# Decode attention with a cache: three loads of the output weights move from ScalarE's DMA queue to SyncE's

## The chip, the core and the metric

The kernel runs on one NeuronCore of one Trainium2 chip. The metric is the device time of one execution in microseconds (us), as the median of several runs. TensorE (PE) does the matmuls, VectorE (DVE), ScalarE (ACT) and GpSimd (POOL) the elementwise work, and SyncE (SP) issues DMAs. ScalarE can issue DMAs too. Each of the two has a DMA queue of its own, and both queues are served by the same 16 DMA engines.

## The reference

32 sequences of 4 new tokens each attend to a cache of 2048 positions. There are 32 query heads of 128 elements, and 4 key and value heads, each shared by 8 query heads. All data are bfloat16.

```python
B, Sq, D = 32, 4, 1024
Hq, Hkv, Sk, Dh = 32, 4, 2048, 128
def reference(x, k_cache, v_cache, wq, wo):
    q = (x @ wq).reshape(B, Sq, Hq, Dh).transpose(0, 2, 1, 3)
    k = jnp.repeat(k_cache, 8, axis=1)
    v = jnp.repeat(v_cache, 8, axis=1)
    scores = jnp.einsum("bhqd,bhkd->bhqk", q, k) * (Dh ** -0.5)
    p = softmax(scores, axis=-1)
    o = jnp.einsum("bhqk,bhkd->bhqd", p, v)
    return o.transpose(0, 2, 1, 3).reshape(B, Sq, Hq * Dh) @ wo
```

The caches are 64 MiB each, wq and wo 8 MiB each; the result y is 128 rows of 1024.

## The kernel before

Three stages follow one another. First x and the four loads of wq come in, and TensorE computes all queries. Then a loop goes over the 32 batches: 2 MiB of keys and 2 MiB of values are loaded, VectorE transposes the keys (`kt`, L333), TensorE computes the scores (`pe_qk`, L346 and the helper at L16) and, three batches later, the weighted values (`pe_pv`, L399, 64 matmuls); ScalarE does the exponentials (L359) and the scaling of the result into `QT_sb` (`o_evac`, L408). Last comes the output projection: VectorE turns the results into `oT_sb` (`o_turn`, L415), TensorE multiplies them with wo head by head (`oproj`, 32 heads, each in three matmuls of 512, 288 and 224 columns: the first of a head is at L425, the others at L16; for the last two heads the 512 columns come first and the rest after), VectorE and ScalarE copy the sums to `y_sb` (L437, L439), and two DMAs store the halves of y (L444), the first issued by SyncE, the second by ScalarE.

A small program object, `_Program`, keeps one list of operations for each engine. An operation stands in its engine's list in the order in which the Python code adds it, with the semaphores that it waits for; an engine does its list strictly in order. So SyncE's list is x, wq, then all loads of keys and values in the order of the list `loads` (L211), then loads of wo (L228), then the first store.

The loads of keys and values go to seven slots of the tensor `big`, four for values and three for keys. wo is loaded into four of these slots once they are free: heads 0 to 7, 8 to 15 and 16 to 23 into the slots of the keys of batches 29, 30 and 31, free when VectorE has transposed these keys (`("kt", b, 1)`), and heads 24 to 31 into the slot of the values of batch 28, free when TensorE has used them (`("pv", 28)`). The loads, `pieces`, are numbered 0 to 13 by the variable `c`: six of four heads (1 MiB), two of two heads, two of one head, and four halves of a head for the last two heads.

Which queue a load of wo takes is chosen at L228:

```python
load = ("act" if c in (1, 3, 5) else "sp", lambda e, dst=dst, src=src: e.dma_start(dst, src),
        [("kt", b, 1) if kind == "k" else ("pv", b)], ("wo", c), f"s_wo{c}")
```

Loads 1, 3 and 5 are kept aside in `act_loads`, and are added to ScalarE's list in the batch loop, right after the scaling of batch 30 (`o_evac(j)` with `j == L - 1`, where `L` is 31). The others are added to SyncE's list behind all loads of keys and values. In `oproj` each matmul waits for the load that brings its weights, `("wo", piece)`, and for the last `o_turn`.

Of the kernel before, what the change touches and what calls it, by code (L numbers as in the profile page):

```python
# [103 lines left out]
def bass_standalone__gqa_block_cached__sampling_kernel(  # L104
# [41 lines left out]
    with ExitStack() as es:  # L146
# [31 lines left out]
        def ps_q(j):  # L178
            return ps_s[:, 512 * j:512 * (j + 1)] if j < 4 else ring[j - 4]

        def words(ap):
            return ap.bitcast(F32)

        p = _Program()
# [18 lines left out]
        for kind, b in loads:  # L203
# [6 lines left out]
            src = (k_cache if kind == "k" else v_cache)[b].rearrange("g (r t) d -> (g r) t d", r=R)  # L210
# [4 lines left out]
        def wo_at(u, m):  # L215
            return big[:, wo_slot[u // 8], :, :].rearrange("p t d -> p (t d)")[:, u % 8 * D:(u % 8 + m) * D]
# [1 line left out]
        wo_v = wo.rearrange("(h p e) n -> p h (e n)", p=128, e=4)  # L218
        pieces = [(sum(WO[:c]), m, 0, D) for c, m in enumerate(WO)] + [(Hq - 2, 1, 0, NA), (Hq - 1, 1, 0, NA), (Hq - 2, 1, NA, D), (Hq - 1, 1, NA, D)]
        assert sum(WO) == Hq - 2  # L220
        act_loads = []
        for c, (u, m, n0, n1) in enumerate(pieces):
            assert u // 4 == (u + m - 1) // 4
            kind, b = wo_for[u // 8]
            dst, src = wo_at(u, m), wo_v[:, u // 4, u % 4 * D:(u % 4 + m) * D]
            if m == 1:
                dst, src = dst[:, n0:n1], src[:, n0:n1]
            load = ("act" if c in (1, 3, 5) else "sp", lambda e, dst=dst, src=src: e.dma_start(dst, src),  # L228
                    [("kt", b, 1) if kind == "k" else ("pv", b)], ("wo", c), f"s_wo{c}")
            if c in (1, 3, 5):  # L230
                act_loads.append(load)
            else:
                p.dma(*load)


        p.op("pool", lambda e: e.memset(ident[:], 0.0), [], "ident0")
# [17 lines left out]
        def pe_idle(n, out_, rhs, waits=()):  # L254
            for c in range(n):
                if c == 0:
                    mm = lambda e: e.matmul(out_, lhsT=ident[:, :], rhs=rhs, start=True, stop=True, skip_group_check=True)  # L257
                else:
                    mm = lambda e: _matmul_held(
                        nc, e, out_, ident[:, :], rhs, tile_size=(128, 128), tile_position=(0, 0), start=True, stop=True)  # L260
                p.op("pe", mm, waits if c == 0 else [])
# [17 lines left out]
        for n, j in enumerate(QJ):  # L279
            g, y = j // 2, j % 2  # L280
            dst = q_sb.rearrange("p (x y) a g e -> p x y a g e", y=2)[:, :, y, :, g, :]
            src = ps_q(j).rearrange("p (h a e) -> p h a e", h=4, a=2)
# [8 lines left out]
        for m in range(4):  # L291
# [6 lines left out]
            for a in range(2):  # L298
                src = ring[m].rearrange("p (h a b s) -> p h a b s", h=2, a=2, b=B)[:, :, a, 0:QB, :]
                dst = words(QT_sb[:, 0:QB, a, 2 * m:2 * m + 2, :, :].rearrange("p b h s w -> p b h (s w)"))  # L300
                dst = dst.rearrange("p b h s -> p h b s")
                p.op("dve", lambda e, s=src, d=dst: e.tensor_copy(d, s), [("qt", m)], ("qa", m, a))  # L302
        for m in range(4):
            for a in range(2):
                src = ring[m].bitcast(BF16).rearrange("p (h a b s) -> p h a b s", h=2, a=2, b=B)[:, :, a, QB:, :]
                dst = QT_sb[:, QB:, a, 2 * m:2 * m + 2, :, :].rearrange("p b h s w -> p h b (s w)")
# [20 lines left out]
        def kt(i, chunks):  # L327
            for c in chunks:
                ts = slice(KC * c, KC * (c + 1))
                src = words(big[:, slot_of("k", i), ts, :].rearrange("p t d -> p (t d)"))  # L330
                dst = words(KT_sb[:, i % 2, ts, :, :, :].rearrange("p t a r w -> p (t a r w)"))
                waits = [("k", i)] + ([("qk", i - 2)] if i > 1 else ["qt_all"] if i == 1 else [])
                p.op("dve", lambda e, s=src, d=dst: e.transpose(d, s), waits, ("kt", i, c), gives="t_kt" if c else None)  # L333

        def pe_qk(i):
            waits = [] if i else [("qs", j) for j in range(8)]
            takes = [("t_kt", 1), ("t_pool", 1)] + [("t_exp", 1)] * (i > 0)
            for a in range(2):
                for w in range(2):
                    for c in range(NCH):  # L340
                        out_ = ps_s[:, 512 * c:512 * (c + 1)]
                        lhsT = QD_sb[:, i % 2, a, :, :, w].rearrange("p g q -> p (g q)")
                        rhs = KT_sb[:, i % 2, TC * c:TC * (c + 1), a, :, w]
                        first, last = (a, w) == (0, 0), (a, w) == (1, 1)
                        if c == 0:
                            mm = lambda e, a_=(out_, lhsT, rhs), f=first, l=last: e.matmul(  # L346
                                a_[0], lhsT=a_[1], rhs=a_[2], start=f, stop=l, skip_group_check=True)
                        else:
                            mm = lambda e, a_=(out_, lhsT, rhs), f=first, l=last: _matmul_held(
                                nc, e, *a_, tile_size=(128, 128), tile_position=(0, 0), start=f, stop=l)  # L350
                        p.op("pe", mm, waits, ("qk", i) if last and c == NCH - 1 else None, takes)
                        waits, takes = [], []

        def softmax_max(i):
            p.op("dve", lambda e: e.tensor_reduce(  # L355
                negmx[:, i % 4:i % 4 + 1], ps_s[:, :], AX.X, ALU.max, negate=True), [("qk", i)], ("negmx", i))

        def softmax_exp(i):
            p.op("act", lambda e: e.activation(  # L359
                P_sb[:, :, :, :].rearrange("p t r w -> p t w r"), ps_s[:, :].rearrange("p (t w r) -> p t w r", w=2, r=R),  # L360
                ACT.Exp, bias=negmx[:, i % 4:i % 4 + 1], accum_out=ssum[:, i % 4:i % 4 + 1]),
                [("negmx", i)] + ([("pt", i - 1)] if i else ["qproj"]), ("exp", i))
            p.give("act", ("exp", i), "t_exp")

        def pt(i):
            src = words(P_flat)
            dst = words(PT_sb[:, i % PB, :, :, :].rearrange("p t q w -> p (t q w)"))
            p.op("dve", lambda e: e.transpose(dst, src), [("exp", i)], ("pt", i))  # L368

        def pe_sum(i):  # L370
            p.op("pe", lambda e: e.matmul(ring[(i if i == L else i // 2 * 2) % 4][:, 510 + i % 2:511 + i % 2], lhsT=permf[:, :], rhs=ssum[:, i % 4:i % 4 + 1], start=True, stop=True),  # L371
                 ["permf"] if i == 0 else [], ("ss", i), [("t_exp", 1)] * (i == L))

        def recip(i):
            n = 1 if i >= L - 1 else 2
            src = ring[i % 4][:, 510 + i % 2:510 + i % 2 + n]
            p.op("dve", lambda e: e.reciprocal(rinv[:, i % 4:i % 4 + n], src), [("ss", i + n - 1)], ("rinv", i))
            if n == 2:
                p.at["rinv", i + 1] = p.at["rinv", i]
# [24 lines left out]
        def o_evac(i):  # L404
            buf = ring_of["o", i]
            dst = QT_sb[:, i, :, :, :, :].rearrange("p a h s w -> p (a h s w)").rearrange("p (a d w) -> p a d w", a=2, w=2)
            src = buf[:, 0:Dh].rearrange("p (d a w) -> p a d w", a=2, w=2)
            p.op("act", lambda e: e.activation(dst, src, ACT.Copy, scale=rinv[:, i % 4:i % 4 + 1]), [("pv", i), ("rinv", i)], ("o", i))  # L408
# [38 lines left out]
        L = B - 1  # L447
# [8 lines left out]
        for i in range(B + LAG):  # L456
            j = i - LAG
            starts.append(len(p.ops["pe"]))
            if i < L:
                kt(i + 1, (0,))  # L460
            if i < B:
                pe_qk(i)
                softmax_max(i)
            if 0 < i < B:
                pe_sum(i - 1)
            if i < B:
                pe_idle(20 if i < LAG else 5, ring[j % 4][:, 0:IDLE], idle_rhs, [("qb", 3, 1), ("qs", 3)] if i == 0 else [])
                softmax_exp(i)
            if 0 < i < B and i % 2 == 0:
                recip(i - 2)  # L470
            if i == L:
                recip(L - 1)
            if i < L:
                kt(i + 1, (1,))
            if i < B:
                pt(i)
            if j >= 0:
                for t in range(T):
                    pe_pv(j, t)
                if i == B:  # L480
                    pe_sum(L)
                o_evac(j)
                if j == L - 1:
                    for load in act_loads:
                        p.dma(*load)
            if i == B:
                recip(L)
            if 0 < i <= B:
                pd(i - 1)
            if i + 2 < B:  # L490
                qd(i + 2)
# [65 lines left out]
```

## Time and profile before

| what | value |
|---|---|
| median of 3 runs | 366.52 us (365.57, 366.52, 366.57) |
| the profiled execution | 366.52 us |
| its span, from the first instruction to the last | 364.7 us |
| busy: PE, DVE, ACT, POOL | 308.2, 269.5, 102.6, 165.3 us |
| mean DMA rate over the span | 416 GB/s |
| bytes read from HBM | 151.26 MB |
| loads of wo issued by SyncE | 11 |
| loads of wo issued by ScalarE | 3, 1024 KB each, median 13.7 us to landing |

All times of events are counted from the start of the span. A row of the timeline has the start, the length, the engine, the line, the operation, the tiles (written <- read), the count, and in brackets the idle time of the engine before it and what ended it. "SPq" and "ACTq" are the DMA issues of SyncE and ScalarE; their length is the time of issuing, not of the transfer. A row of the table by stretches has the window, its length, then the busy time and the count of instructions of PE, of PE's weight loads, DVE, ACT and POOL, then the granted clock of TensorE (1.00 is full speed), the busy share of the DMA engines and the rate.

### The profile page before, as it was taken

Reading aid. Unit: us, or ns where it says so; the run is one execution under the profiler, and the core shown is the slowest. Engines: PE = TensorE matmul, PEld = TensorE weight load, DVE = VectorE, ACT = ScalarE, POOL = GpSimd, SP = SyncE. Lnnn points to the kernel's source line nnn. Section 1 sums busy time; section 2 is a strip of 40 time slices with the busy share of each in tenths; the row PEclk is TensorE's granted clock in tenths of the full one; section 3 lists DMA queues with packets and bytes.
Section 4 is the critical chain, followed back from the end, with each engine's and each line's share of the span. In section 5 each row is a group of like instructions: output and inputs, shape, how many; then the busy total and the mean of one; then the engine's idle time right before and its main releaser. Section 6 shows DMA issues by size and latency. Waiting matters only on the chain. (4 is left out here: it accounts for less than half of the span.)

```text
span 364.7 us, 6248 instructions
## 1 busy us (share of the span) xinstructions
PE 308.2 (85%) x3030; PEld 147.2 (40%) x2340; DVE 269.5 (74%) x171; ACT 102.6 (28%) x110; POOL 165.3 (45%) x262
## 2 busy tenths in 40 slices
PE   1988788999999999988998888888888888899586
PEld 1002000445544555544544444444444433469411
DVE  0018799998899999879999888888888888856201
ACT  1014222333333333333333333333332332223000
POOL 8002055355555555555555544444445555543000
PEclk9999999999999999999999999999999999999989
DMA  8999999999999999999999999999999999999992
GB/s 325 431 431 428 426 429 429 431 429 426 423 426 426 429 429 424 430 431 428 431 426 429 423 429 426 429 429 431 428 431 428 428 431 424 426 429 419 420 407 75
DMA packets 12251, 151.66 MB, mean 416 GB/s; under 512 B 1360, under 2 KB 2128, under 8 KB 2768
## 3 DMA queue, kind: packets, MB, share of 16 engines
q1 hardware_dynamic: 11664, 148.25, 95.9%
q10 hardware_dynamic: 576, 3.28, 2.2%
q8 instruction: 6, 0.10, 0.1%
q14 instruction: 5, 0.04, 0.0%
HBM read 151.26 MB, written 0.26 MB: 415 GB/s over the span
## 5 line engine op out<-in xcount | busy, mean ns | idle before, releaser
L333 DVE STREAM_TRANSPOSE KT_sb<-big 128x2048 f32<-128x2048 f32 x64 | 146.6, 2293 | 16.1 <-DMA big<-in_k_cache_dram 16.1
L359 ACT ACTIVATE P_sb<-ps_s,negmx 128x2048 bf16<-128x2048 f32 x32 | 82.1, 2566 | 184.5 <-DVE negmx L355 184.5
L16 PE MATMUL ps_s<-KT_sb,QD_sb 128*128 128x512 bf16 x384 | 103.7, 377 | 0.0
L390 POOL COPY PD_sb<-PT_sb 32x1024 f32<-32x1024 f32 x62 | 64.1, 1034 | 63.2 <-PE ps_r L399 60.4
L390 POOL COPY big<-PT_sb 32x1024 f32<-32x1024 f32 x61 | 63.0, 1034 | 58.7 <-PE ps_r L399 56.0
L355 DVE TENSOR_REDUCE negmx<-ps_s 128x1 f32<-128x2048 f32 x32 | 73.2, 2288 | 12.4 <-PE ps_s L16 10.8
L399 PE MATMUL ps_r<-big 128*128 128x128 bf16 x1024 | 59.8, 219 | 11.6 <-PEq L85 11.6
L399 PE MATMUL ps_r<-big,PD_sb 128*128 128x128 bf16 x1024 | 59.8, 219 | 9.9 <-PEq L85 9.9
L399 PEld LDWEIGHTS ps_r<-big 128*128 128x128 bf16 x1024 | 57.9, 98 | 22.3 <-issue 21.9
L399 PEld LDWEIGHTS ps_r<-big,PD_sb 128*128 128x128 bf16 x1024 | 58.0, 98 | 21.1 <-issue 20.6
L346 PE MATMUL ps_s<-KT_sb,QD_sb 128*128 128x512 bf16 x128 | 48.3, 377 | 17.9 <-PEq L85 17.9
L346 PEld LDWEIGHTS ps_s<-KT_sb,QD_sb 128*128 128x128 bf16 x128 | 12.4, 96 | 102.6 <-issue 102.6
L368 DVE STREAM_TRANSPOSE PT_sb<-P_sb 128x1024 f32<-128x1024 f32 x32 | 39.8, 1245 | 15.8 <-ACT P_sb L359 15.8
L323 POOL COPY QD_sb<-QT_sb 32x64 f32<-32x64 f32 x128 | 29.4, 230 | 46.3 <-DVE QT_sb L302 20.6
L16 PE MATMUL ps_r<-ident 128*128 128x384 bf16 x173 | 33.3, 325 | 0.0
L371 PEld LDWEIGHTS ps_r<-ssum,permf 128*128 128x128 f32 x64 | 11.9, 187 | 24.8 <-issue 23.1
L408 ACT ACTIVATE QT_sb<-ps_r,rinv 128x128 bf16<-128x128 f32 x32 | 11.7, 367 | 29.7 <-PE ps_r L399 27.5
L284 DVE TENSOR_SCALAR KT_sb<-ps_r 128x512 bf16<-128x512 f32 x2 | 1.3, 686 | 20.2 <-PE ps_r L268 20.2
L425 PE MATMUL ps_s<-big,KT_sb 128*128 128x512 bf16 (+1 forms) x32 | 12.6, 405 | 3.3 <-DMA big<-in_wo_dram 3.3
L439 DVE CAST P_sb<-ps_s 128x512 bf16<-128x512 f32 (+1 forms) x2 | 1.0, 536 | 18.9 <-PE ps_s L425 18.9
L16 PE MATMUL ps_s<-big,KT_sb 128*128 128x224 bf16 (+1 forms) x62 | 12.9, 291 | 1.2 <-DVE KT_sb L415 1.1
L257 PE MATMUL ps_r<-ident 128*128 128x384 bf16 x32 | 10.3, 322 | 0.0
(41 smaller groups left out, 85.1 us busy)
## 6 DMA issues: line engine op xcount, KB each, us to landing
big<-in_k_cache_dram SPq DMA_DIRECT2D x32, 2048.0 KB, 18.5
big<-in_v_cache_dram SPq DMA_DIRECT2D x32, 2048.0 KB, 22.0
big<-in_wq_dram SPq DMA_DIRECT2D x4, 2048.0 KB, 14.2
big<-in_wo_dram SPq DMA_DIRECT2D x3, 1024.0 KB, 21.1
big<-in_wo_dram ACTq DMA_DIRECT2D x3, 1024.0 KB, 13.7
big<-in_wo_dram SPq DMA_DIRECT2D x2, 512.0 KB, 23.7
big<-in_wo_dram SPq DMA_DIRECT2D x2, 256.0 KB, 25.1
big<-in_wo_dram SPq DMA_DIRECT2D x4, 128.0 KB, 23.4
```

Source lines behind the costliest of these rows:

```text
L16: return eng.add_instruction(mybir.InstMatmult(name=nc.get_next_instruction_name(), engine=eng.engine, start_tensor_calc=start, stop_tenso ...
L323: p.op("pool", lambda e, s=src, d=dst: e.tensor_copy(d, s), waits if g == 0 else [("pt", i - 2)] * (g == 1 and i > 1), ("qd", i) if g == G ...
L333: p.op("dve", lambda e, s=src, d=dst: e.transpose(d, s), waits, ("kt", i, c), gives="t_kt" if c else None)
L346: mm = lambda e, a_=(out_, lhsT, rhs), f=first, l=last: e.matmul(a_[0], lhsT=a_[1], rhs=a_[2], start=f, stop=l, skip_group_check=True)
L355: p.op("dve", lambda e: e.tensor_reduce(negmx[:, i % 4:i % 4 + 1], ps_s[:, :], AX.X, ALU.max, negate=True), [("qk", i)], ("negmx", i))
L359: p.op("act", lambda e: e.activation(P_sb[:, :, :, :].rearrange("p t r w -> p t w r"), ps_s[:, :].rearrange("p (t w r) -> p t w r", w=2, r=R),
L368: p.op("dve", lambda e: e.transpose(dst, src), [("exp", i)], ("pt", i))
L371: p.op("pe", lambda e: e.matmul(ring[(i if i == L else i // 2 * 2) % 4][:, 510 + i % 2:511 + i % 2], lhsT=permf[:, :], rhs=ssum[:, i % 4:i ...
L390: p.op("dve" if i >= B - 2 and g < i - B + 4 else "pool", lambda e, s=src, d=dst: e.tensor_copy(d, s), [free] * (g == 0 or i >= B - 2) + [ ...
L399: p.op("pe", lambda e: e.matmul(buf[:, 0:Dh], lhsT=pd_of(i)[:, t // 2, :, :, :, t % 2].rearrange("p x g q -> p (x g q)"), rhs=big[:, slot_ ...
L408: p.op("act", lambda e: e.activation(dst, src, ACT.Copy, scale=rinv[:, i % 4:i % 4 + 1]), [("pv", i), ("rinv", i)], ("o", i))
L425: mm = lambda e, a=(out_, lhsT, rhs): e.matmul(a[0], lhsT=a[1], rhs=a[2], start=(u == 0), stop=(u == Hq - 1), skip_group_check=True)
```

## The change

The three loads 1, 3 and 5 are issued by SyncE, in their places between the others, and ScalarE's list no longer has them. What each load waits for, where it writes and who waits for it stay the same. The store of the second half of y is issued by ScalarE in both kernels.

```diff
-        act_loads = []
         for c, (u, m, n0, n1) in enumerate(pieces):
             assert u // 4 == (u + m - 1) // 4
             kind, b = wo_for[u // 8]
             dst, src = wo_at(u, m), wo_v[:, u // 4, u % 4 * D:(u % 4 + m) * D]
             if m == 1:
                 dst, src = dst[:, n0:n1], src[:, n0:n1]
-            load = ("act" if c in (1, 3, 5) else "sp", lambda e, dst=dst, src=src: e.dma_start(dst, src),
-                    [("kt", b, 1) if kind == "k" else ("pv", b)], ("wo", c), f"s_wo{c}")
-            if c in (1, 3, 5):
-                act_loads.append(load)
-            else:
-                p.dma(*load)
+            p.dma("sp", lambda e, dst=dst, src=src: e.dma_start(dst, src),
+                [("kt", b, 1) if kind == "k" else ("pv", b)], ("wo", c), f"s_wo{c}")
...
                 o_evac(j)
-                if j == L - 1:
-                    for load in act_loads:
-                        p.dma(*load)
```

## The prediction

> **What bounds the kernel now.** I read the chain that ended last on the page first, then the chain for the last 29 us, then the timeline, the clock and transfer table and the DMA issues for the same stretch. The chain of 336 to 365 us:
>
> ```profile
> by line: DMA big<-in_wo_dram 35.7%; PE ps_s L425 23.6%; PE ps_s L16 23.0%; PE ps_r L399 4.9%; DVE P_sb L439 2.4%; DVEq L146 1.0%; issue 0.5%; ACT QT_sb L408 0.0%
> ...
> 337.44 10.36 DMA big<-in_wo_dram
> ```
>
> The longest piece is one load of wo that ScalarE issues at 337.44 and that lands 10.36 us later, at 347.8. The timeline says who waits for it:
>
> ```profile
> 322.47 18.74 SPq L228 DMA_DIRECT2D big<-in_wo_dram  x11
> ...
> 337.44 1.37 ACTq L228 DMA_DIRECT2D big<-in_wo_dram  x3
> ...
> 342.92 0.38 PE L16 MATMUL ps_s<-big,KT_sb 128*128 128x288 bf16 x2 [1.10 <-DVE KT_sb L415]
> ...
> 347.85 0.39 PE L425 MATMUL ps_s<-big,KT_sb 128*128 128x512 bf16 x1 [3.25 <-DMA big<-in_wo_dram]
> ```
>
> TensorE begins the output projection at 342.9, does the four heads of the first load, and stands still for 3.25 us until the second load, ScalarE's first, has landed. The table by stretches (us, busy time and count of each engine, granted clock, DMA share, GB/s) shows what follows:
>
> ```profile
> 13.70:27.00 13.30, 11.73 (x54) 0.68 (x7) 1.39 (x3) 1.17 (x3) 0.00 (x0) 1.00 1.01 434
> ...
> 338.00:340.90 2.90, 2.82 (x51) 2.85 (x52) 1.17 (x3) 0.00 (x0) 0.00 (x0) 1.00 1.02 427
> 340.90:344.80 3.90, 2.59 (x28) 1.12 (x18) 0.30 (x2) 0.37 (x1) 0.00 (x0) 1.00 1.01 416
> 344.80:348.20 3.40, 0.35 (x3) 0.10 (x1) 0.00 (x0) 0.00 (x0) 0.00 (x0) 1.00 1.02 422
> 348.20:351.60 3.40, 3.40 (x15) 0.59 (x5) 0.00 (x0) 0.00 (x0) 0.00 (x0) 0.50 1.02 419
> 351.60:355.30 3.70, 3.70 (x26) 0.90 (x9) 0.00 (x0) 0.00 (x0) 0.00 (x0) 0.99 0.99 390
> 355.30:358.00 2.70, 2.65 (x19) 0.59 (x6) 0.00 (x0) 0.00 (x0) 0.00 (x0) 1.00 0.58 200
> ```
>
> The stretch after the pause has a granted clock of 0.50: 3.4 us of work done at half speed costs a further 1.7 us. TensorE never waits again and ends last, while the DMA engines are full (share about 1) only until 355 and empty at 358. So the tail pays 3.25 + 1.7 = 4.95 us, not because bytes are missing, but because they come in the wrong order: while the second load is outstanding, SP's queue brings loads that are needed later. The DMA view of 342 to 344 shows the two queues sharing equally:
>
> ```profile
> q10 hardware_dynamic: 51, 0.42, 50.1%
> q1 hardware_dynamic: 57, 0.40, 48.1%
> ```
>
> q10 is ScalarE's queue (it has nothing before 340 us), q1 SP's.
>
> **What is removed and moved.** Number the loads of wo 0 to 13. Loads 1, 3 and 5 (1 MB each, heads 4-7, 12-15, 20-23) go from ScalarE to SP, each between its neighbours. The store of the second half of y is on ScalarE's queue in both kernels; the diff leaves it alone.
>
> On ScalarE three issues go (1.37 us from 337.44). They lie between the scaling of batch 30 and that of batch 31 at 341.85, which waited for TensorE, so that saves nothing.
>
> On SP three issues are added. Its row is 0.43 us for one (issue starts 322.47, 322.94 and 323.42): 3 x 0.47 = 1.4 us. They fall behind load 0 at 322.47 and end by about 325.3. The slots they write were read out by the transposes of keys 29 to 31, the last of which ended at 320.4, so they don't wait. Load 6 waits for the values of batch 28 until 330.09, and SP stands idle before it:
>
> ```profile
> SPq L228 <- PE ps_r L399: 6.2, 1, 6.2
> ```
>
> So the 1.4 us hides in 6.2 us; with that cover gone it would still stand some 15 us ahead of the first landing that could feel it. Nothing of k or v stands behind these issues.
>
> SP then meets a fuller queue. Three of its late issues take far longer than 0.43 us: those that start at 332.71, 335.39 and 337.54 take 2.64, 2.10 and 3.67 us. About ten loads are then issued and not landed (v of batches 30 and 31 and eight of wo at 332.71). With three more ahead, this begins at load 8 (331) instead of load 11. If each later issue waits for one landing, loads 8 to 13 go out at about 333, 338, 340, 343, 345 and 348. The last one's data are wanted at 357.8, so 10 us are spare: cost nothing.
>
> **When each load lands.** The value rows of batch 31 land at 322.10 + 15.8 = 337.9 and load 0 at 322.47 + 17.8 = 340.3; neither changes, as what stands ahead of them doesn't. From 340.3 the queue brings the loads in order. The rate is the row of 338 to 340.9, where SP's queue alone brings rows of this size: 427 GB/s, 2.46 us per 1,048,576 bytes. For the last six loads I keep the steps between landings of before (issue start plus time to landing gives 355.3, 355.9, 356.6, 357.0, 357.3, 357.6, 357.9 for loads 7 to 13). TensorE's pace is one head per 0.434 us (352.58, 353.01, 353.44 in the timeline), a start 0.05 us after a landing (347.80 to 347.85).
>
> | load | heads | lands | TensorE free | starts |
> |---|---|---|---|---|
> | 0 | 0-3 | 340.3 | 342.9 | 342.9 |
> | 1 | 4-7 | 342.8 | 344.7 | 344.7 |
> | 2 | 8-11 | 345.2 | 346.4 | 346.4 |
> | 3 | 12-15 | 347.7 | 348.1 | 348.1 |
> | 4 | 16-19 | 350.1 | 349.9 | 350.2 |
> | 5 | 20-23 | 352.6 | 351.9 | 352.6 |
> | 6, 7 | 24-27 | 353.8, 355.1 | 354.4 | 354.4 |
> | 8, 9 | 28, 29 | 355.8, 356.4 | 356.1 | 356.1 |
> | 10, 11 | 30, 31, first 512 columns | 356.8, 357.1 | 357.0 | 357.2 for 31 |
> | 12, 13 | 30, 31, the rest | 357.4, 357.75 | 357.4 | 357.8 for 31 |
>
> Both limits meet at the end: without any wait TensorE would start that last piece at 356.6, and the loads allow 357.8. What is late next is therefore the transfer itself.
>
> ```profile
> 361.46 0.99 DVE L439 CAST P_sb<-ps_s 128x512 bf16<-128x512 f32 x2 [18.90 <-PE ps_s L425]
> 361.48 0.29 PE L425 MATMUL ps_s<-big,KT_sb 128*128 128x288 bf16 x1
> ...
> 362.53 0.35 ACTq L444 DMA_DIRECT2D out_dram<-P_sb  x1
> ```
>
> Before, that last piece starts at 361.48: 3.7 us later. The first 512 columns of head 31 go from about 361.2 to 357.2, 4.0 us. The second store waits for two casts in a row on VectorE, of which the first follows the 512 columns: I take 3.9. The profiled execution took 366.52 us, which is the median itself: a span of 364.7 and 1.8 around it. 366.52 - 3.9 = 362.6.
>
> Bounds of the one unknown, the rate of one queue: at the whole span's mean of 416 GB/s the 7.34 MB after load 0 take 0.5 us longer (363.1); at 390, the row of 351.6 to 355.3, 1.6 us longer (364.2). A faster queue ends at TensorE's own limit, 361.48 - 356.6 = 4.9 less: 361.6.
>
> [...]
>
> For the clock my row is the first stage. From 13.7 to 27 us TensorE waits for a load twice (0.26 and 1.26 us), is busy 88%, and keeps a granted clock of 1.00. The table above has pauses of at most 0.7 us and some 90% busy.
>
> **The rivals.**
> *Half clock stays.* If waiting for loads 4 and 5 brings a spell of 0.50, 3.4 us of work cost 1.7 more: 364.3, and less where TensorE then waits for the loads anyway. For it: the spell at 348.2. Against: that followed 3.25 us without one matmul. 8%.
> *One queue is slower than two.* No gain if the loads end at 361.3 instead of 357.75: 7.34 MB in 21.0 us, 350 GB/s. Then about 366.5. For it: 200 GB/s in the last stretch, where rows are short and the engines run dry. Against: 427 with one queue and 416 to 422 with two. 6%.
> *SP's full queue stalls the loads (slower).* Place: issues 8 to 13. If a blocked issue went on only when the queue is empty, each of the six would cost a lone transfer's time, 1.75 us (the stores' issue to landing), from load 7's 355.1: 365.6 instead of 357.75, so 370.5. It decides once load 13 is issued later than about 356; for: the issues of 2.1 to 3.7 us; against: the DMA share stayed at 1 while they were blocked. 6%.
> *It doesn't do what it says* is no case: the store doesn't move, and the three loads do.
>
> **How the numbers follow.** A difference of 0.3% (1.1 us; three runs of before spread over 1.0) is about what a measurement here tells from none. The forecast has 80%, with its own range 361.6 to 364.2. Faster: forecast and half clock, 0.88; same 0.06; slower 0.06. The range takes in the rate's bounds and the half clock, with half the spread of the runs at either end: 361.2 to 364.7. It leaves out the last two cases, 12%.
>
> **What would show it.** Right: no pause before head 4; no 0.50 between 343 and 358; q10 with only the store's 0.13 MB; load 1 landing near 342.8; SP's long issues beginning near 331; TensorE waiting for wo in short pieces after 350; the DMA engines still empty near 358 and the last matmul within half a microsecond of that. Wrong: a DMA share under 1 between 340 and 355, or a clock of 0.50 after 344.

## The result, and the profile after

The median falls from 366.54 us (6 runs, 365.57 to 366.79) to 363.05 us (6 runs, 362.96 to 363.14). The ratio is 0.9909, with a 95% interval from 0.9897 to 0.9922: 3.5 us less, where 3.9 were forecast. The profiled execution took 362.99 us, with a span of 361.2. One run of the kernel before, among those beside the experiments, took 638.79 us, far from all others, and is left out of every figure below.

First the DMA queues in the profile of the kernel after (queue: packets, MB, share):

```profile
q1 hardware_dynamic: 12096, 151.39, 99.0%
...
q10 hardware_dynamic: 144, 0.13, 0.1%
```

ScalarE's queue (q10) is left with the second store alone. Load 1 is now issued at 323.03. Its row among the DMA issues gives 19.8 us to landing, so it lands at 342.8, not at 347.8:

```profile
big<-in_wo_dram SPq DMA_DIRECT2D x1, 1024.0 KB, 19.8
```

The table by stretches, in the same stretches as before (us; busy time and count of PE, its weight loads, DVE, ACT, POOL; granted clock, DMA share, GB/s):

```profile
340.90:344.80 3.90, 2.79 (x31) 1.29 (x20) 0.30 (x2) 0.37 (x1) 0.00 (x0) 1.00 1.01 416
344.80:348.20 3.40, 3.40 (x26) 0.78 (x8) 0.00 (x0) 0.00 (x0) 0.00 (x0) 1.00 1.01 422
348.20:351.60 3.40, 2.89 (x20) 0.64 (x7) 0.00 (x0) 0.00 (x0) 0.00 (x0) 1.00 1.00 414
351.60:355.30 3.70, 3.12 (x22) 0.63 (x7) 0.00 (x0) 0.00 (x0) 0.00 (x0) 1.00 1.02 396
355.30:358.00 2.70, 2.70 (x19) 0.68 (x7) 0.19 (x1) 0.00 (x0) 0.00 (x0) 1.00 0.57 195
```

From 344.8 to 348.2 TensorE is busy for 3.40 us, where it was busy for 0.35. The clock stays at 1.00. The DMA columns are nearly those of before: the engines were full then and are full now. Only the order of the bytes is different. The timeline shows the waits that are left, and the end (the new kernel is shorter: its L420, L434 and L439 are L425, L439 and L444 of before):

```profile
350.33 0.39 PE L420 MATMUL ps_s<-big,KT_sb 128*128 128x512 bf16 x1 [0.46 <-DMA big<-in_wo_dram]
...
352.82 0.39 PE L420 MATMUL ps_s<-big,KT_sb 128*128 128x512 bf16 x1 [0.57 <-DMA big<-in_wo_dram]
...
358.04 0.30 PE L420 MATMUL ps_s<-big,KT_sb 128*128 128x288 bf16 x1
...
358.95 0.37 ACTq L439 DMA_DIRECT2D out_dram<-P_sb  x1
```

The last weights (load 13, issued at 346.58, 11.4 us to landing) land at 358.0. TensorE starts the piece that needs them at 358.04 (361.48 before), and the second store is issued at 358.95 (362.53 before). The tail now hangs on the transfer: TensorE works almost without a pause behind load 5, which lands at 352.8, and its last piece waits for load 13. The chain that ended last says the same. TensorE's part has shrunk from 9% of the span to 2%, and the largest part is now a load of wo, load 5 (from its issue at 324.92 on, so its time in the queue is counted). The first row is from before, the others from after:

```profile
PE 9%; DMA 3%; DVE 0%; DVEq 0%; issue 0%; ACT 0%
...
DMA 8%; PE 2%; SPq 1%; DVE 0%; issue 0%
DMA big<-in_wo_dram 8%; PE ps_r L394 1%; PE ps_s L420 1%; PE ps_s L16 1%; SPq L227 1%; DVE P_sb L434 0%; SPq L211 0%
```

### The profile page after: what moved, and what is told of

The parts are those of the page before. It is cut to its first block, busy times and chain, and to the rows that moved or that the text cites. A ratio compares the mean times of both kernels' runs of the same rounds, so it can differ in the third digit from the quotient of the medians.

```text
span 361.2 us, 6248 instructions
## 1 busy us (share of the span) xinstructions
PE 307.2 (85%) x3030; PEld 147.0 (41%) x2340; DVE 269.4 (75%) x171; ACT 102.6 (28%) x110; POOL 165.4 (46%) x262
## 5 line engine op out<-in xcount | busy, mean ns | idle before, releaser
L279 DVE TENSOR_SCALAR KT_sb<-ps_r 128x512 bf16<-128x512 f32 x2 | 1.3, 686 | 19.8 <-PE ps_r L263 19.8
L16 PE MATMUL ps_s<-big,KT_sb 128*128 128x224 bf16 (+1 forms) x62 | 12.0, 272 | 1.2 <-DVE KT_sb L410 1.1
L420 PE MATMUL ps_s<-big,KT_sb 128*128 128x512 bf16 (+1 forms) x32 | 11.8, 375 | 1.0 <-DMA big<-in_wo_dram 1.0
L434 DVE CAST P_sb<-ps_s 128x512 bf16<-128x512 f32 (+1 forms) x2 | 1.1, 542 | 15.2 <-PE ps_s L420 15.2
```

The source lines that it names most:

```text
L16: return eng.add_instruction(mybir.InstMatmult(name=nc.get_next_instruction_name(), engine=eng.engine, start_tensor_calc=start, stop_tenso ...
L420: mm = lambda e, a=(out_, lhsT, rhs): e.matmul(a[0], lhsT=a[1], rhs=a[2], start=(u == 0), stop=(u == Hq - 1), skip_group_check=True)
```

## The experiments

The theory under test: what counts is the order in which the bytes of wo come through full DMA engines; a second queue breaks that order. The rivals: ScalarE's queue is slower by itself; or ScalarE only issues too late; or the half clock is the whole loss. All five kernels start from the kernel before.

**Only load 1 goes back.**

```diff
-            load = ("act" if c in (1, 3, 5) else "sp", ...
-            if c in (1, 3, 5):
+            load = ("act" if c in (3, 5) else "sp", ...
+            if c in (3, 5):
```

> Only load 1 of wo goes back to SP; loads 3 and 5 stay on ScalarE's queue. Theory (order: two busy queues share equally, so a load that is needed soon gets half the rate beside one that is needed later): load 1 lands near 344.6 and the pause before head 4 is gone, but load 2 now shares with load 3 and lands near 349.5, so TensorE pauses about 3.1 us before head 8; time 364.8 without a spell of half clock, up to 366.5 with one. Rival (the trouble is only that load 1 waits for ScalarE, whose first issue is at 337.4): with load 1 back the whole gain is there, 363.

Measured: 366.19 us (12 runs, 364.75 to 367.73), 0.9989 of before (0.9973 to 1.0006): the gain isn't there. The pause has moved to head 8, as the timeline of this kernel shows, and its table shows a half clock after it:

```profile
349.52 0.61 PE L425 MATMUL ps_s<-big,KT_sb 128*128 128x512 bf16 x1 [3.04 <-DMA big<-in_wo_dram]
```

```profile
344.80:348.70 3.90, 1.68 (x12) 0.29 (x3) 0.00 (x0) 0.00 (x0) 0.00 (x0) 1.00 1.03 426
348.70:355.50 6.80, 5.98 (x22) 1.17 (x8) 0.00 (x0) 0.00 (x0) 0.00 (x0) 0.50 1.01 400
```

Load 2 is issued at 323.59 and lands 25.9 us later, at 349.5, the figure expected; load 1 lands at 344.5. The rival (only load 1 matters) falls: it asked for 363. Load 3, which ScalarE brings, lands at 347.9, before its heads are due, while load 2, which is due first, lands 4.2 us later than in the kernel after (345.3). This profiled run is the slowest of the twelve, with 6.8 us of half clock. The four runs with a mean granted clock of 1.000 took 364.75 to 365.21, those at 0.995 365.88 to 367.01. So even at full clock this order costs about 1.9 us against the 363.05 of the kernel after.

**The pause filled with matmuls that nothing uses.** The order of the loads stays that of before.

```diff
         for u in range(Hq - 2):
+            if u == 4:
+                pe_idle(18, ring[0][:, 0:IDLE], idle_rhs)
             oproj(u, (0, 1, 2))
```

> The kernel before, with 18 matmuls that nothing uses (128x384, 0.163 us each, 2.9 us) put on TensorE between heads 3 and 4, where it pauses. Theory: the clock stays at 1.00, heads 4 to 31 take 0.434 us each from 347.85, with waits for loads 3 and 5 (351.6, 355.3); the end is about 1.2 us earlier: 365.3. The rest of the gain of the change, 2.3 us, is the order of the loads. Rival (the half clock costs nothing, since TensorE would wait for loads anyway): 366.5.

Measured: 365.39 us (12 runs, 365.25 to 365.84), 0.9976 of before (0.9962 to 0.9990). Its timeline and table:

```profile
344.40 2.93 PE L16 MATMUL ps_r<-ident 128*128 128x384 bf16 x17
347.85 0.39 PE L425 MATMUL ps_s<-big,KT_sb 128*128 128x512 bf16 x1 [0.53 <-DMA big<-in_wo_dram]
```

```profile
348.20:351.60 3.40, 3.30 (x24) 0.69 (x7) 0.00 (x0) 0.00 (x0) 0.00 (x0) 1.00 1.02 419
```

Load 1 lands when it did, head 4 starts when it did, but the next 3.4 us run at a clock of 1.00 with 24 matmuls in place of 15. That is worth 1.1 us of the median (366.48 for the kernel before in the same comparison). The other 2.3 to 2.4 of the change are the order itself.

The runs of the kernel before say the same. Beside the experiments, those with a mean granted clock of 0.999 or 1.000 took 365.27 to 365.68 us, those at 0.995 366.10 to 366.86, those at 0.991 367.64 to 367.93. The profiled execution, at 0.995, has one spell of 3.4 us. So the order costs 2.4 us in every run, and on top of that come 0, 1.0 or 2.3 us of half clock, which differ from run to run.

**All loads on ScalarE's queue, in order.**

```diff
-            load = ("act" if c in (1, 3, 5) else "sp", ...
-            if c in (1, 3, 5):
-                act_loads.append(load)
-            else:
-                p.dma(*load)
+            load = ("act", ...
+            act_loads.append(load)
...
-                if j == L - 1:
-                    for load in act_loads:
+                if j >= L - 1:
+                    for load in (act_loads[:8] if j == L - 1 else act_loads[8:]):
```

> All 14 loads of wo in order on ScalarE's queue: 0 to 7 after the scaling of batch 30 (337.4), 8 to 13 after that of batch 31. Theory (order decides, not which queue): each load lands in order at the rate of the kernel after, with one gap of about 1 us, because load 0 is issued at 337.4 and not early; all landings about 1 us later than in the kernel after: 364.0 (363.5 to 364.6), no half clock. Rival (ScalarE's queue is slower by itself): 366 or more.

Measured: 367.20 us (12 runs, 366.68 to 367.59), 1.0018 of before (1.0003 to 1.0032). That is the rival's number, and 3 us above the theory's. The table of its profile shows why:

```profile
334.00:336.00 2.00, 2.00 (x40) 2.00 (x38) 1.90 (x3) 0.24 (x1) 0.94 (x1) 1.00 0.88 369
336.00:336.50 0.50, 0.50 (x13) 0.50 (x11) 0.47 (x2) 0.00 (x0) 0.00 (x0) 1.00 0.31 131
336.50:338.00 1.50, 1.10 (x20) 0.92 (x17) 1.47 (x2) 0.36 (x1) 0.00 (x0) 1.00 0.08 33
338.00:339.00 1.00, 0.90 (x17) 0.94 (x18) 1.00 (x2) 0.00 (x1) 0.00 (x0) 1.00 0.42 66
339.00:340.00 1.00, 1.00 (x22) 1.00 (x20) 0.37 (x3) 0.00 (x0) 0.00 (x0) 1.00 0.65 213
340.00:342.00 2.00, 1.83 (x33) 1.65 (x30) 0.00 (x0) 0.03 (x1) 0.00 (x0) 1.00 1.00 422
```

The engines run empty from 336 on, stand nearly still until 338, and are full again only at 340. From 336 the shares missing from 1 add up to 2.7 us, and the missing rate, against the 422 GB/s of the last row, to 3.1 us; 0.3 us more is missing from 334 to 336. The expectation had 1. It counted the gap from the landing of the last values (338.0), but these thin out before: their last packet of 16 KB starts at 336.86 and ends at 337.5. Load 0 is issued at 337.64, its first packets start at 338.7, and they come slowly until 340. Once it runs, the queue is as fast as SP's: 422 GB/s, where SP's brings loads 2 to 5 of the kernel after at 421. The landings lag those of the kernel after by 3.6 us at load 1, of which the gap makes up 3.3 to 3.4, and by 4.4 at load 13. The 0.8 us that is added lies between loads 5 and 6, which land 2.1 us apart (1.3 in the kernel after); why stays open. As far as this run alone goes, the rival isn't refuted, so the next kernel takes the gap away.

**All loads on ScalarE's queue, the first eight one batch earlier.**

```diff
-                if j >= L - 1:
-                    for load in (act_loads[:8] if j == L - 1 else act_loads[8:]):
+                if j in (L - 2, L):
+                    for load in (act_loads[:8] if j == L - 2 else act_loads[8:]):
```

> As the kernel with all loads of wo on ScalarE's queue, but loads 0 to 7 are issued one batch earlier, after the scaling of batch 29 (333.7 to 337.4), so that the DMA engines don't run empty between the last values and load 0; 8 to 13 still after that of batch 31. Theory (order and an unbroken stream decide, not the queue): loads land in order as in the kernel after, the last near 358.0; the last values land up to 0.5 us later because two queues share for 2 us; 363.2 (362.9 to 363.9). Rival (ScalarE's queue is slower by itself, or its issues hold up the scaling): 366 or more, as with the issue at 337.4.

Measured: 363.63 us (6 runs, 363.12 to 364.50), 0.9925 of before (0.9899 to 0.9951), within 0.6 us of the kernel after. Its stretches and queues:

```profile
336.00:336.50 0.50, 0.50 (x12) 0.50 (x10) 0.47 (x2) 0.00 (x0) 0.00 (x0) 1.00 0.70 295
336.50:338.00 1.50, 1.12 (x20) 0.94 (x17) 1.47 (x2) 0.00 (x0) 0.00 (x0) 1.00 0.98 404
338.00:340.00 2.00, 1.54 (x28) 1.57 (x29) 1.21 (x2) 0.00 (x0) 0.00 (x0) 1.00 1.00 377
340.00:342.00 2.00, 2.00 (x40) 2.00 (x37) 0.30 (x2) 0.37 (x1) 0.00 (x0) 1.00 1.03 430
```

```profile
q10 hardware_dynamic: 2160, 8.52, 5.9%
```

All 8.4 MB of wo come by q10, in order and without a gap but for a dip in the half microsecond from 336, and nearly the whole gain is there. The last load lands at 358.4, 0.4 us later than in the kernel after. So ScalarE's queue is not slower here (430 GB/s from 340 to 342); what the kernel before lacks is order.

**The three loads on ScalarE's queue, 15 us earlier.**

```diff
-                if j == L - 1:
+                if j == L - 4:
                     for load in act_loads:
```

> Loads 1, 3 and 5 stay on ScalarE's queue but are issued 15 us earlier, after the scaling of batch 27 (322.5). Theory (order; the DMA engines are full, so what is brought early pushes back what is needed first): these 3 MB take half the rate from the values of batches 29 to 31, the last of which land near 345 in place of 338; TensorE waits there and starts the output projection near 350: 369 to 371, slower than before. Rival (the loads on ScalarE's queue come late only because they are issued late): 363.

Measured: 367.72 us (9 runs, 367.14 to 369.37), 1.0049 of before (1.0026 to 1.0072). Slower, as the theory has it and against the rival, but 1.3 us less than the lower end expected. Load 1 now lands at 333.5, long before it is needed, so a late landing of that load is not the trouble here. The timeline shows TensorE waiting ahead of the 64 matmuls with the values of batch 31, which land at 343.65 (the row names only PE's own sequencer, PEq). The first row is from before, the second from this run; the DMA view of 328 to 334 us of this run shows how the queues share:

```profile
338.08 3.73 PE L399 MATMUL ps_r<-big 128*128 128x128 bf16 x64 [0.68 <-PEq L85]
...
343.79 3.73 PE L399 MATMUL ps_r<-big 128*128 128x128 bf16 x64 [2.11 <-PEq L85]
```

```profile
q1 hardware_dynamic: 123, 1.79, 70.2%
q10 hardware_dynamic: 119, 0.84, 33.6%
```

In these 6 us the two queues got nearly the same number of packets (123 and 119), not of bytes (1.79 and 0.84 MB): the rows of values are 16 KB a packet, those of wo 8 KB, so the values kept some 70% of the time. My half and half was too harsh: the last values land at 343.7, not 345, and the projection starts at 348.4, not 350. The run shows that these loads can also be issued too early. Whether a time between 322 and 337 would do as well for these three loads as one queue does was not tried.

## Why the prediction was right

*The bound.* Right in kind: a pause for load 1 and the half clock behind it, not a lack of bytes. The price of 3.25 + 1.7 = 4.95 us was too high. The experiments found 2.4 us for the order and 1.0 to 1.1 for a spell of half clock: at full clock, as the run with the filled pause shows, heads 12 and 20 must wait for loads 3 and 5 (they start at 351.6 and 355.4). The forecast did not rest on that price but on the times at which the loads land. It took the profiled execution, with one spell, as the standard. The median run of before also has one, as 25 of the 42 runs beside the experiments do; against the 10 at full clock the gain is 2.4 us, not 3.5.

*The order of landing.* Right. Loads 1 to 5 were put at 342.8, 345.2, 347.7, 350.1 and 352.6 and landed at 342.8, 345.3, 347.8, 350.3 and 352.8.

*The rate: the term that was mis-sized.* From load 1 to load 5 a load takes 2.49 us (9.95 us for four), 421 GB/s, not 427. The last one lands at 358.0 instead of 357.75, and the last piece starts at 358.04 instead of 357.8. Load 11, wanted by the first 512 columns of head 31, lands at 357.34 instead of 357.1, and these columns start at 357.39 instead of 357.2. In the profile of before they start at 361.04, not at the "about 361.2" of the prediction, so the gain there is 3.65 us and not 4.0: half of that miss is the rate, half the reading. The first cast gains the same 3.65 (357.81), and the second store 3.58 instead of 3.9. That is 0.3 of the miss of 0.45 us; the rest is spread over steps of less than 0.1 us, among them the difference between the profiled executions and the medians.

*SP's queue.* Right in cost, a little early in time. The waits of SP's queue show that the idle time before load 6 fell from 6.2 by the three issues:

```profile
SPq L227 <- PE ps_r L394: 4.8, 1, 4.8
```

Long issues begin at load 7 (330.54, 1.19 us), and one takes longer than any of before:

```profile
340.26 6.28 SPq L227 DMA_DIRECT2D big<-in_wo_dram  x1
```

The last issue starts at 346.58 and ends at 348.7 (348 was said), over 9 us ahead of its landing. The DMA share is 1.00 or more in every stretch from 338 to 355.3, so the slower rival had no place: the issue of 6.28 us held up SP alone, which had nothing else to do.

*The clock.* Right. The waits for loads 4 and 5 (0.46 and 0.57 us) leave it at 1.00. All six runs of the kernel after have a mean clock of 0.999 or 1.000 and lie within 0.18 us.

No version beats the kernel after in these runs: its DMA engines are full until 355, and what remains behind the last landing is 3.2 us of one head's matmuls, casts and a store.

## What to carry to other kernels

In this kernel one queue kept the DMA engines full (share 1.02 and 427 GB/s from 338 to 340.9 us of the kernel before), and so did two (1.01 to 1.02, 416 to 422 GB/s from 340.9 to 351.6). The second queue brought no bytes earlier; it only mixed two orders. For a stretch that looks the same: put loads on one queue in the order in which they are needed, early enough that the engines never run empty (empty engines cost the run with all loads on ScalarE's queue some 3 us), and look in the trace for a pause whose load was issued late or shared its stretch with loads that are needed later. Count a half clock behind a pause of TensorE as a cost of its own: behind the 3.25 us of the kernel before it was 1.0 to 1.1 us a spell, which came in some runs and not in others.

## What the runs showed of the hardware

With both queues busy, nearly equal counts of packets were seen on SP's and ScalarE's queue in three places: at equal rows (57 to 51 in 342 to 344 us of before, with 8 KB each), at 16 KB against 8 KB (123 to 119 in 328 to 334 us of the run with the three loads 15 us earlier, 70% to 34% of the time), and late in the kernel before, when SP's queue had rows of 4 KB and ScalarE's of 8 KB. The DMA view of 348 to 352 us of the kernel before:

```profile
q10 hardware_dynamic: 152, 1.11, 66.9%
q1 hardware_dynamic: 150, 0.55, 34.3%
```

So in the last two the queue with the longer rows took the larger share of the time. The counts were not equal throughout: from 353 to 353.5 us of the kernel before, SP's queue moved 39 packets (0.10 MB) and ScalarE's 18 (0.10 MB).

Spells of half clock were 3.4 us long in the kernel before (a granted clock of 0.50 from 348.2 to 351.6) and 6.8 in the run with one load moved back (0.50 from 348.7 to 355.5), and came in some runs only: by their mean clock, in 32 of the 42 runs of the kernel before beside the experiments, and in none of the 12 with the pause filled by matmuls. What else sets them off, no run shows. The profiles show that TensorE had not stood still for all of the 3.4 us ahead of a spell: they held 0.37 us of matmuls in the kernel before (344.81 to 348.22), 0.92 in the run with the three loads 15 us earlier (332.84 to 336.25; the clock is 0.54 from 336 to 339.7) and 1.16 in the run with load 1 moved back (345.32 to 348.72).

The last load landed 0.4 to 0.5 us after its last packet: in the kernel after, load 13 has its last packet at 357.6 and its landing at 358.0, and in the kernel before, its last packets end by 357.5 and it lands at 357.9.

In the kernel before, the load on the second queue starts late beside a full first one. Load 1 is issued at 337.44, and q10's first packets start at 341.0, 3.6 us later. The DMA views of 338 to 340.9 and of 340.9 to 341.1 us:

```profile
q1 hardware_dynamic: 173, 1.24, 102.3%
...
q10 hardware_dynamic: 2, 0.02, 19.9%
```

In the run with all loads on ScalarE's queue, where the engines are nearly empty (a share of 0.08 from 336.5 to 338), load 0 takes 1.0 us from its issue to its first packets (337.64 to 338.7). Why a full first queue goes with a later start, no run shows. So of the 10.4 us that load 1 takes in the kernel before, 3.6 pass ahead of its first packet, while SP's queue brings load 0 and begins load 2. How much of the 2.4 us this late start causes, and how much the sharing behind it, the runs do not separate; that sharing alone can cost as much as 1.9 us is shown by the run with load 1 moved back.
